# A transformer block on one core: the first queries from scaled weights, late rows and early modulates retimed, and attention's k, v and wq loads two steps later

## The chip, the cores and the metric

One NeuronCore of one Trainium2 chip. The metric is device time in microseconds (us). Engines: TensorE (PE; PEld is its weight load), VectorE (DVE), ScalarE (ACT), GpSimd (POOL), and SyncE (SP), whose instruction queue issues nearly all DMAs here.

## The reference, cut to what matters

```python
def reference(A_x, A_k_cache, A_v_cache, A_wq, A_wo, B_x, B_w_in, B_w_sp, B_b_sp, B_w_out, c, w_mod):
    mod = (_silu(c) @ w_mod).reshape(c.shape[0], 6, 1, -1)      # w_mod is (1024, 6144)
    sa, ca, ga, sb, cb, gb = ...                                 # six rows of 1024
    h = _layernorm(x) * (1 + ca) + sa                            # x is (1, 2048, 1024)
    x = x + ga * attention(h)       # q = h @ wq; 32 heads of 128; k and v cached, 2048 keys; @ wo
    h = _layernorm(x) * (1 + cb) + sb
    x = x + gb * gated_mlp(h)       # GELU, layernorm, token mixing by w_sp, w_out
    return x
```

All tensors are bf16. Before the first query exists the kernel needs x normalised, the columns sa and 1 + ca (a 4 MB part of w_mod times one vector), and wq.

## The kernel before

Attention runs as 64 "halves" of 16 steps: a half is one head and 1024 of the 2048 queries, a step is 128 keys. Halves 0 to 15 take heads 0 to 7 (first 1024 queries of each, then the rest); later, two halves per head. Each step is two score matmuls, one exponential on ScalarE, two matmuls with v, and a running sum `pacc` on VectorE, with one matmul of the next queries as filling. The first 1024 rows of x are normalised, transposed and modulated before attention; the other eight rows of tiles ("late rows") are done on VectorE during halves 0 to 6.

```python
    load_wm(nc.scalar, 0, 1)                       # w_mod in 512 KB blocks of 256 columns
    load_wm(nc.scalar, 1, 1)
    for ti in range(8):
        nc.sync.dma_start(xg[ti // 2][:, ti % 2], x_dram[:, ti, :])
    load_wm(nc.sync, 0, 0)
    ...                                            # k0, more w_mod, wq and v, mixed
    def q_work(h, qh, new_ps=side_ps):             # queries of one half, in 16 matmuls
        ...
                nc.tensor.matmul(box["ps"][:], wq_t[:, dc, hc:hc + DH],
                                 h1T[:, dc, q0:q0 + 512],
                                 start=(dc == 0), stop=(dc == KD - 1))
    ...
    def late_rows(g):                              # g counts steps from 0 to 1023
        ti, r = 8 + (g - 4) // 12, (g - 4) % 12
        if g == 0:
            load_row(8)
        if 4 <= g < 100:
            if r == 0:   ...                       # statistics of one row of tiles, next load
            elif r == 2: ...                       # normalise, store
            elif r == 6: ...                       # load back transposed, into h1T
        elif 100 <= g < 108:
            modulate(g - 100, 1024, 1024)
    ...
    for g, (i, kb) in enumerate(steps):            # i is the half, kb the step in it
        ...
        if kb == 2 and i < 16:
            load_kv(halves[i + 1][0])              # kT (a DMA transpose) and v
            if i == 12:
                load_wq(2)                         # 1 MB
        elif kb == 2 and qh == 0 and h + 1 < H:
            load_kv(h + 1)
            if h % 4 == 2 and h + 2 < H:
                load_wq((h + 2) // 4)
        ...                                        # the matmuls, the exponential, the sum
        if i > 0:
            work = ({13: finish_here, 15: load_rec} if i <= 8 else
                    {0: store_sums, 3: turn_sums, 10: finish_den, 13: load_rec}).get(kb)
            if work:
                work(i - 1)                        # the softmax denominators of the half before
```

From half 9 on, the denominators take a way through DRAM: the sums are stored (step 0), loaded back by a DMA transpose as `pT` (`turn_sums`, step 3), reduced on VectorE as `den` (`finish_den`, step 10), and their reciprocals go out and come back broadcast as `rbc`.

The softmax here doesn't subtract the row's maximum and nothing guards it: scores larger than these inputs give would overflow.

Of the kernel before, what the change touches and what calls it, by code (L numbers as in the profile page):

```python
# [16 lines left out]
def kernel(  # L17
# [42 lines left out]
    def wide_ps(name, shape=(P, 1024), dtype=FP32):  # L60
        return psum.tile(list(shape), dtype, name=name, tag="wide", bufs=2)

    def bank_ps(name, shape, dtype=FP32):
        return psum.tile(shape, dtype, name=name, tag="bank", bufs=3)
# [35 lines left out]

    c_sb = early.tile([KD, P], BF16, name="c_sb")
    nc.sync.dma_start(c_sb[:], c.rearrange("o (kc p) -> (o kc) p", p=P))
    xg, wms = [], []
    for j in range(4):
        xg.append(early.tile([P, 2, D], BF16, name=f"xg{j}"))
        wms.append(early.tile([P, 2, KD, 256], BF16, name="wm", tag="wm", bufs=4))

    def load_wm(eng, j, k):
        eng.dma_start(wms[j][:, k], wmod_v[:, :, k * D + j * 256:k * D + (j + 1) * 256])


    k0 = early.tile([P, NKB, DH], BF16, name="k0")
# [4 lines left out]
    kts[0] = att.tile([P, S], BF16, name="kT", tag="kT", bufs=2)  # L117
    vs[0] = att.tile([P, NKB, DH], BF16, name="v_sb", tag="v_sb", bufs=2)
    nc.scalar.activation(small.tile([P, 1], FP32, name="warm_e")[:], eps_tile[:], ACT.Exp)
    load_wm(nc.scalar, 0, 1)  # L120
    load_wm(nc.scalar, 1, 1)
    for ti in range(8):
        nc.sync.dma_start(xg[ti // 2][:, ti % 2], x_dram[:, ti, :])
    load_wm(nc.sync, 0, 0)
    load_wm(nc.sync, 1, 0)
    nc.sync.dma_start(k0[:], A_k_cache[0, 0].rearrange("(p j) d -> p j d", p=P))
    load_wm(nc.sync, 2, 0)
    nc.sync.dma_start(wq_g[0][:, :, 0:256], wq_v[:, :, 0:256])
    load_wm(nc.sync, 3, 0)
    nc.sync.dma_start(vs[0][:], A_v_cache[0, 0].rearrange("(p j) d -> p j d", p=P))  # L130
    nc.sync.dma_start(wq_g[0][:, :, 256:512], wq_v[:, :, 256:512])

    def ln_stats(chunks):

# [34 lines left out]
    def silu():  # L169

        nc.tensor.transpose(cT_ps[:], c_sb[:, :], identity[:KD, :KD])
        nc.scalar.activation(e_sb[:], cT_ps[:], ACT.Exp, scale=-1.0)
        load_wm(nc.scalar, 2, 1)
        load_wm(nc.scalar, 3, 1)

    def silu_end():
        nc.vector.tensor_scalar_add(out=e_sb[:], in0=e_sb[:], scalar1=1.0)
# [11 lines left out]

    mpss = {}  # L190

    def mod_products(j):
        mps = mpss[j] = bank_ps("mps", [P, 2, 2])
        for k in range(2):
            for f in range(2):
                for kc in range(KD):
                    nc.tensor.matmul(mps[:, k, f:f + 1], wms[j][:, k, kc, f * P:(f + 1) * P],
                                     scT[:, kc:kc + 1], start=(kc == 0), stop=(kc == KD - 1))

    def mod_columns(j):  # L200
        mps = mpss.pop(j)
        nc.vector.tensor_copy(out=cols[:, 0, 2 * j:2 * j + 2], in_=mps[:, 0, :])
        nc.vector.tensor_scalar_add(out=cols[:, 1, 2 * j:2 * j + 2], in0=mps[:, 1, :],
                                    scalar1=1.0)

    def modulate(dc, t0, n, eng=nc.vector, src=None):

        dst = h1T[:, dc, t0:t0 + n]
        if src is None:
            src = dst  # L210
        else:
            dst = dst.rearrange("p (t k) -> p t k", k=P)
        if eng is nc.scalar:
            nc.scalar.activation(dst, src, ACT.Identity, bias=cols[:, 0, dc:dc + 1],
                                 scale=cols[:, 1, dc:dc + 1])
            return
        nc.vector.tensor_scalar(out=dst, in0=src, scalar1=cols[:, 1, dc:dc + 1],
                                scalar2=cols[:, 0, dc:dc + 1], op0=ALU.mult, op1=ALU.add)

    row, junk = {}, early.tile([P, D], BF16, name="junk")  # L220

    def stats_act(ti):

# [19 lines left out]
        nc.gpsimd.tensor_tensor(out=rstd[:], in0=var[:], in1=neg_half[:], op=ALU.pow)  # L243
        row[ti] = (mv, rstd)

    turned_x = {}

    def turn(j, evacuate=True):
        hps = turned_x[j] = wide_ps("hps", [P, KD, 2, P], BF16)
        for t in range(2):  # L250
            for dc in range(KD):
                nc.tensor.transpose(hps[:, dc, t, :],
                                    xg[j][:, t, dc * P:(dc + 1) * P], identity[:])
        if evacuate:
            nc.scalar.activation(
                h1T[:, :, j * 256:(j + 1) * 256],
                hps[:].rearrange("p d t k -> p d (t k)"), ACT.Copy)

    def dve(ti):
        row[ti] = row_stats(xg[ti // 2][:, ti % 2, :])  # L260
# [20 lines left out]
    norm(1)  # L281
    turn(0)
    keep_busy(4)
    mod_products(0)
    finish_act(2)
    stats_act(5)
    dve(4)
    norm(2)
    norm(3)
    turn(1)  # L290
    mod_columns(0)
    mod_products(1)
    keep_busy(4)
    dve(6)
    norm(4)
    finish_act(5)
    dve(7)
    norm(5)
    turn_k(0)
    turn(2)  # L300
    mod_columns(1)
    mod_products(2)
    norm(6)
    norm(7)
    turn(3, False)
    k_late = turn_k(1, False)
    keep_busy(2)
    mod_products(3)
    mod_columns(2)
    for dc in range(4):  # L310
        modulate(dc, 0, 768)
    for dc in (4, 5):
        modulate(dc, 0, 768)
        modulate(dc, 768, 256, nc.scalar, turned_x[3][:, dc, :, :])
    mod_columns(3)
    modulate(6, 0, 768)
    modulate(7, 0, 768, nc.scalar)
    for dc in range(4):
        modulate(dc, 768, 256, nc.vector, turned_x[3][:, dc, :, :])
    for dc in (6, 7):  # L320
        modulate(dc, 768, 256, nc.scalar, turned_x[3][:, dc, :, :])
    k_late()


    wo_v = A_wo.rearrange("(h p) n -> p h n", p=P)
# [13 lines left out]
    def q_work(h, qh, new_ps=side_ps):  # L339

        out_t = att.tile([P, 1024], BF16, name="qT", tag="qT", bufs=3)
        qts[(h, qh)] = out_t
        wq_t = wq_g[h // 4]
        hc = (h % 4) * DH
        work = []
        for j in range(2):
            box = {}

            def one(dc, j=j, box=box):
                if dc == 0:  # L350
                    box["ps"] = new_ps("qps", [P, 512])
                q0 = qh * 1024 + j * 512
                nc.tensor.matmul(box["ps"][:], wq_t[:, dc, hc:hc + DH],  # L353
                                 h1T[:, dc, q0:q0 + 512],
                                 start=(dc == 0), stop=(dc == KD - 1))
                if dc == KD - 1:
                    nc.vector.tensor_copy(out=out_t[:, j * 512:(j + 1) * 512],  # L357
                                          in_=box["ps"][:])
            for dc in range(KD):
                work.append(lambda dc=dc, one=one: one(dc))  # L360
        return work


# [14 lines left out]
        s_tiles[g] = sps  # L378

    nc.sync.dma_start(wq_g[1][:], wq_v[:, :, 512:1024])  # L380
    for fn in q_work(0, 0, bank_ps):
        fn()
    emit_s(0)
    emit_s(1)
# [86 lines left out]

    def late_rows(g):

        ti, r = 8 + (g - 4) // 12, (g - 4) % 12
        if g == 0:
            load_row(8)
        if 4 <= g < 100:
            if r == 0:
                rows[ti] += row_stats(rows[ti][0][:, :]),
                if ti + 1 < NT:  # L480
                    load_row(ti + 1)
            elif r == 2:
                xt, st = rows.pop(ti)
                hb = early.tile([P, D], BF16, name="hb1", tag="hb1", bufs=2)
                centre(xt[:, :], st, hb[:])
                nc.sync.dma_start(h1_dram[ti % 2], hb[:])
            elif r == 6:
                nc.sync.dma_start(out=h1T[:, :, ti * P:(ti + 1) * P], in_=h1_dram[ti % 2],
                                  transpose=True)
        elif 100 <= g < 108:  # L490
            modulate(g - 100, 1024, 1024)

    def load_row(ti):
        rows[ti] = (early.tile([P, D], BF16, name="xt", tag="xt", bufs=2),)
        nc.sync.dma_start(rows[ti][0][:], x_dram[:, ti, :])

    wm_l = {}
    cols_l = early.tile([P, 32], FP32, name="cols_l")

    def late_mods(i, kb):  # L500
# [1 line left out]

        n0, odd = divmod(i - 17, 2)
        if n0 < 8 and not odd and kb == 2:
            wm_l[n0] = early.tile([P, KD, 512], BF16, name="wm_l", tag="wm", bufs=4)
            nc.sync.dma_start(wm_l[n0][:], wmod_v[:, :, (n0 + 4) * 512:(n0 + 5) * 512])
        elif n0 < 8 and not odd and kb == 14:
            wm = wm_l.pop(n0)
            mod_ps = side_ps("mod_ps", [P, 4])
            for f in range(4):  # L510
                for kc in range(KD):
                    nc.tensor.matmul(mod_ps[:, f:f + 1], wm[:, kc, f * P:(f + 1) * P],
                                     scT[:, kc:kc + 1], start=(kc == 0), stop=(kc == KD - 1))
            nc.vector.tensor_scalar_add(out=cols_l[:, 4 * n0:4 * n0 + 4], in0=mod_ps[:],
                                        scalar1=1.0 if n0 // 2 == 2 else 0.0)
        elif i == 33 and kb == 2:
            turned = early.tile([P, 32], FP32, name="turned_l")
# [12 lines left out]
    for g, (i, kb) in enumerate(steps):  # L530
# [10 lines left out]
        if kb == 2 and qh == 1 and 20 <= h < 28:  # L541
            k = 4 * (h - 20)
            nc.sync.dma_start(wo_t[:, k:k + 4, :], wo_v[:, k:k + 4, :])
        if kb == 2 and i < 16:
            load_kv(halves[i + 1][0])
            if i == 12:
                load_wq(2)
        elif kb == 2 and qh == 0 and h + 1 < H:
            load_kv(h + 1)
            if h % 4 == 2 and h + 2 < H:  # L550
                load_wq((h + 2) // 4)
# [233 lines left out]
```

## Time and profile before

| | |
|---|---|
| time, median of 12 runs | 1871.03 us (1867.56 to 1873.41) |
| span of the profiled run | 1869.1 us |
| TensorE busy | 1831.2 us (98%) |
| first exponential of attention | 32.97 us |
| a half without stalls | 17.29 us (80 matmuls, 216 ns apart) |

I cut attention into halves by the start of each half's first exponential, read from the timeline. Most halves take 17.29 us; eight of the halves 17 to 32 take 18.07 because they also hold 32 small matmuls for later modulation columns. The following stood out:

```
half          2      5      6      12     20     21     28     36     52
us            19.02  19.22  18.19  17.88  21.14  19.05  19.14  18.35  18.17
without stall 17.29  17.29  17.29  17.29  18.07  17.29  18.07  17.29  17.29
```

Four views of the kernel before follow. First, the page: busy us of each engine with its share of the span and instruction count.

```profile
PE 1831.2 (98%) x8830; PEld 845.9 (45%) x8995; DVE 1261.6 (68%) x2110; ACT 1105.0 (59%) x1167; POOL 32.8 (2%) x55
```

Second, the chain of waits around the worst stall (start us, us, what).

```profile
392.24 1.36 SPq L329
393.60 0.05 issue
393.65 10.14 DMA pT<-sums_dram
403.79 0.02 issue
403.81 1.23 DVE den L418
...
406.74 0.38 PE sps L374
```

TensorE's score matmul at 406.74 can be followed back to a DMA of 10.14 us. The issues on the sync queue in that stretch (timeline: start, us, engine, line, operation) say why:

```profile
389.12 0.36 SPq L406 DMA_DIRECT2D sums_dram<-pacc  x1
389.58 1.98 SPq L334 DMA_TRANSPOSE kT<-in_A_k_cache_dram  x1
391.65 0.53 SPq L336 DMA_DIRECT2D v_sb<-in_A_v_cache_dram  x1
392.24 1.36 SPq L329 DMA_DIRECT2D wq_t<-in_A_wq_dram  x1
393.65 4.60 SPq L411 DMA_TRANSPOSE pT<-sums_dram  x1
```

The pT transpose goes out behind kT, v and wq, 2 MB in all. By the completion semaphores in the trace they landed in the order of issue: kT at 393.72, v at 396.04, wq at 401.20 and pT at 403.79. The waits from 190 to 1150 us (total us, times, longest us) say how often this holds VectorE:

```profile
DVE den L418 <- DMA pT<-sums_dram: 15.4, 7, 4.4
```

Seven times, 4.4 us at worst. Third, the start, from the timeline: the last normalise, the last block of w_mod, the column products that wait for it, the first exponential.

```profile
15.51 4.54 SPq L109 DMA_DIRECT2D wm<-in_w_mod_dram  x1
...
21.48 1.16 DVE L151 TENSOR_SCALAR xg<-xg,mv,rstd 128x1024 bf16<-128x1024 bf16 x2
...
27.29 0.95 PE L197 MATMUL mps<-scT,wm 128*128 128x1 bf16 x32 [0.77 <-DMA wm<-in_w_mod_dram]
...
32.97 2.85 ACT L555 ACTIVATE pt<-sps 128x1024 bf16<-128x1024 f32 x3 [0.71 <-PE sps L374]
```

Fourth, windows of halves 0, 1, 20 and 21: length, then busy us (and instructions) of PE, PEld, DVE, ACT and POOL, the granted clock of TensorE, the DMA share and GB/s.

```profile
32.97:50.40 17.43, 16.68 (x76) 7.50 (x77) 12.10 (x21) 15.84 (x17) 0.86 (x1) 1.00 0.44 113
50.40:67.89 17.49, 17.38 (x87) 7.92 (x88) 14.85 (x27) 15.97 (x18) 0.93 (x1) 1.00 0.45 106
386.02:407.16 21.14, 18.03 (x111) 8.55 (x112) 14.47 (x24) 16.17 (x18) 0.00 (x0) 1.00 0.73 162
407.16:426.21 19.05, 19.00 (x81) 8.30 (x81) 16.01 (x27) 16.05 (x17) 0.00 (x0) 0.91 0.41 125
```

In half 21 the granted clock is 0.91: the trace's clock records show half speed from 407.4 to 410.9 us, just after the stall (128x512 matmuls start 427 ns apart there).

### The profile page before, as it was taken

How to read it: one execution, taken by the hardware profiler on the slowest of the kernel's cores; microseconds unless marked ns; L12 is line 12 of the kernel's file. 1: busy time of each engine (PE TensorE's matmuls, PEld its weight loads, DVE VectorE, ACT ScalarE, POOL GpSimd, SP SyncE). 2: the span in 40 equal slices, each digit the busy share in tenths (PEclk: the TensorE clock that was granted, in tenths of full speed). 3: DMA queues.
4: the chain of work that ended last, by engine and by line, in shares of the span. 5: the costliest groups of instructions: out<-in, count | busy, mean ns of one | idle time of the engine just before them, and what ended most of it. 6: DMA issues, size and time to landing. Idle time of an engine off the chain costs nothing.

```text
span 1869.1 us, 24473 instructions
## 1 busy us (share of the span) xinstructions
PE 1831.2 (98%) x8830; PEld 845.9 (45%) x8995; DVE 1261.6 (68%) x2110; ACT 1105.0 (59%) x1167; POOL 32.8 (2%) x55
## 2 busy tenths in 40 slices
PE   6999999999999999999999999999999999999999
PEld 4444444444444444444444444444445444444444
DVE  6898888878888988888888888444455400333334
ACT  6889999988988989999999997000013332000000
POOL 1000000000000000000000000000000000000000
PEclk9999999999999999999999999999999999999999
DMA  8465465464564643564564433766433012221102
GB/s 248 120 169 118 128 156 153 124 153 123 132 172 116 164 122 99 142 167 127 136 167 131 109 108 112 226 206 157 116 88 87 12 46 79 51 56 40 46 1 79
DMA packets 404346, 223.68 MB, mean 120 GB/s; under 512 B 302592, under 2 KB 359936, under 8 KB 404224
## 3 DMA queue, kind: packets, MB, share of 16 engines
q1 hardware_dynamic: 400064, 220.01, 44.3%
q10 hardware_dynamic: 4160, 2.10, 0.4%
q8 instruction: 70, 1.15, 0.3%
q14 instruction: 52, 0.43, 0.1%
HBM read 126.88 MB, written 45.63 MB: 92 GB/s over the span
## 4 chain that ended last, share of the span: by engine, by line
PE 89%; DVE 4%; DMA 4%; issue 1%; SPq 1%; ACT 0%; POOL 0%; DVEq 0%; ACTq 0%; POOLq 0%
PE ops L567 20%; PE sps L374 20%; PE acc L466 12%; PE qps L353 10%; PE gps L714 10%; PE zps L664 5%; PE bo L735 5%; PE zps L697 5%; DMA pT<-sums_dram 3%; DVE pacc L577 2%; DMA wm<-in_w_mod_dram 1%; SPq L329 0%; DVE den L418 0%; DVE qT L357 0%; ACT pt L555 0%
## 5 line engine op out<-in xcount | busy, mean ns | idle before, releaser
L555 ACT ACTIVATE pt<-sps 128x1024 bf16<-128x1024 f32 x1024 | 1018.7, 1025 | 107.8 <-PE sps L374 78.5
L577 DVE TENSOR_TENSOR pacc<-pacc,pt 128x1024 bf16<-128x1024 bf16 x896 | 616.8, 688 | 63.2 <-ACT pt L555 4.0
L374 PE MATMUL sps<-qT,kT 128*128 128x512 bf16 x1999 | 600.3, 379 | 7.9 <-DVE qT L357 6.9
L567 PE MATMUL ops<-pt,v_sb 128*128 128x512 bf16 x1993 | 598.1, 379 | 6.2 <-DVE ou L573 1.3
L353 PE MATMUL qps<-h1T,wq_t 128*128 128x512 bf16 x1022 | 344.2, 380 | 2.1 <-DVE rec L431 1.2
L567 PEld LDWEIGHTS <-v_sb 128*128 128x128 bf16 x2048 | 200.2, 98 | 250.3 <-issue 9.7
L374 PEld LDWEIGHTS <-kT 128*128 128x128 bf16 x2048 | 199.1, 98 | 245.8 <-issue 9.7
L466 PE MATMUL acc<-wo_t,ot 128*128 128x512 bf16 x972 | 215.7, 379 | 1.1
L666 ACT ACTIVATE z<-zps 128x448 bf16<-128x448 f32 x64 | 34.8, 544 | 283.3 <-PE zps L664 280.4
L714 PE MATMUL gps<-wsp,z 128*128 128x512 bf16 x878 | 192.9, 379 | 0.9
L717 DVE TENSOR_TENSOR g<-gps,b_bc 128x512 bf16<-128x512 f32 x56 | 38.7, 692 | 222.1 <-PE gps L714 215.2
L353 PEld LDWEIGHTS <-wq_t 128*128 128x128 bf16 x1024 | 100.2, 98 | 121.2 <-issue 0.8
L466 PEld LDWEIGHTS <-ot 128*128 128x128 bf16 x992 | 97.0, 98 | 116.8
L714 PEld LDWEIGHTS <-z 128*128 128x128 bf16 x896 | 87.7, 98 | 105.7
L357 DVE CAST qT<-qps 128x512 bf16<-128x512 f32 x128 | 88.4, 691 | 42.3 <-PE qps L353 41.2
L735 PE MATMUL bo<-w_out_t,z1T 128*128 128x512 bf16 x439 | 96.7, 379 | 0.5
L664 PE MATMUL zps<-z2w,h2T 128*128 128x448 bf16 x512 | 97.0, 352 | 0.0
L697 PE MATMUL zps<-h2T,z1w 128*128 128x512 bf16 x439 | 96.4, 379 | 0.5
L643 DVE TENSOR_TENSOR tmp<-acc,ga 128x512 f32<-128x512 f32 x32 | 22.0, 688 | 100.2 <-PE acc L466 100.2
L418 DVE TENSOR_REDUCE den<-pT 128x8 f32<-128x1024 bf16 x55 | 65.3, 1187 | 15.4 <-DMA pT<-sums_dram 15.4
L440 DVE TENSOR_TENSOR oT<-ou,rbc 128x1024 bf16<-128x1024 f32 x62 | 75.6, 1219 | 0.2 <-DMA rbc<-rec_dram 0.2
L664 PEld LDWEIGHTS <-h2T 128*128 128x128 bf16 x512 | 50.1, 98 | 46.8
(82 smaller groups left out, 649.3 us busy)
## 6 DMA issues: line engine op xcount, KB each, us to landing
rbc<-rec_dram SPq DMA_DIRECT2D x64, 512.0 KB
v_sb<-in_A_v_cache_dram SPq DMA_DIRECT2D x40, 512.0 KB
oT_dram<-oT SPq DMA_DIRECT2D x62, 256.0 KB
sums_dram<-pacc SPq DMA_DIRECT2D x55, 256.0 KB
ot<-oT_dram SPq DMA_DIRECT2D x24, 512.0 KB
wm_l<-in_w_mod_dram SPq DMA_DIRECT2D x8, 1024.0 KB
wo_t<-in_A_wo_dram SPq DMA_DIRECT2D x8, 1024.0 KB
wq_t<-in_A_wq_dram SPq DMA_DIRECT2D x7, 1024.0 KB
```

Source lines behind the costliest of these rows:

```text
L353: nc.tensor.matmul(box["ps"][:], wq_t[:, dc, hc:hc + DH], h1T[:, dc, q0:q0 + 512], start=(dc == 0), stop=(dc == KD - 1))
L357: nc.vector.tensor_copy(out=out_t[:, j * 512:(j + 1) * 512], in_=box["ps"][:])
L374: nc.tensor.matmul(sps[:, j * 512:(j + 1) * 512], kts[h][:, kb * P:(kb + 1) * P], qts[(h, qh)][:, j * 512:(j + 1) * 512], start=True, stop ...
L440: nc.vector.tensor_mul(out=oT[:], in0=state[i]["ou"][:], in1=state[i]["rbc"][:])
L466: nc.tensor.matmul(accs[ti][:, sl], lhs, wo_t[:, hh, sl], start=(hh == 0), stop=(hh == H - 1))
L555: nc.scalar.activation(pt[:], s_tiles.pop(g)[:], ACT.Exp, scale=SCALE)
L567: nc.tensor.matmul(o_ps[j][:], vs[h][:, kb, :], pt[:, j * 512:(j + 1) * 512], start=(kb == 0), stop=(kb == NKB - 1))
L577: nc.vector.tensor_add(out=pacc[:], in0=pacc[:], in1=pt[:])
L664: nc.tensor.matmul(zps[:], h2T[:, dc, ti * P:(ti + 1) * P], z2w[:, dc, sl], start=(dc == 0), stop=(dc == KD - 1))
L697: nc.tensor.matmul(zps[:], w[:, dc, :], h2T[:, dc, q * 512:(q + 1) * 512], start=(dc == 0), stop=(dc == KD - 1))
L714: nc.tensor.matmul(gps[:], z2[s][:, f * P:(f + 1) * P], wsps[q][:, s, :], start=(s == 0), stop=(s == NT - 1))
L735: nc.tensor.matmul(bo[:], z1T[:, f, ti * P:(ti + 1) * P], w_out_t[:, f, sl], start=(f == 0), stop=(f == NF - 1))
```

## The change

Its intent is to begin attention before the modulation is done. Since (n * (1 + ca) + sa) @ wq = n @ ((1 + ca) * wq) + sa @ wq, the first two heads' queries of the first 1024 rows are made from unmodulated rows `xnT` with scaled weights `wqs`, and the shift `q_add` is added when the result is copied out of PSUM, the buffer that the matmuls write. The rows that later heads need are modulated in steps 2 to 9 of half 0. w_mod comes in 1 MB blocks of 512 columns behind x; `keep_busy(n)` issues n dummy matmuls on zeros, whose result nobody uses, to keep TensorE busy; the late rows start at step 14 and follow every 11 steps; and the k, v and wq loads of attention move from step 2 to step 4 of a half.

```diff
-    load_wm(nc.scalar, 0, 1)
-    load_wm(nc.scalar, 1, 1)
     for ti in range(8):
         nc.sync.dma_start(xg[ti // 2][:, ti % 2], x_dram[:, ti, :])
-    load_wm(nc.sync, 0, 0)
-    load_wm(nc.sync, 1, 0)
+    nc.sync.dma_start(wq_g[0][:, :, 0:256], wq_v[:, :, 0:256])
     nc.sync.dma_start(k0[:], A_k_cache[0, 0].rearrange("(p j) d -> p j d", p=P))
     ... (the rest of w_mod, v and wq are issued after the small exponential of silu)
+    def scale_wq(j):
+        for dc in range(4 * j, 4 * j + 4):
+            ... (wqs = wq * (1 + ca): four on ScalarE, four on VectorE)
+    def query_shift():
+        ... (16 matmuls of one column: qs = wq^T sa; q_add = qs)
     ... (start of attention)
-    turn(3, False)
-    k_late = turn_k(1, False)
-    keep_busy(2)
+    turn(3, (0, 1))
+    scale_wq(0)
+    turn_k(1)
+    keep_busy(4)
     mod_products(3)
-    ... (16 modulates on VectorE and ScalarE)
+    mod_columns(3)
+    scale_wq(1)
+    keep_busy(8)
+    mod_products(0)
+    mod_columns(0)
     ...
-    for fn in q_work(0, 0, bank_ps):
+    first = q_work(0, 0, bank_ps)
+    for fn in first[:7]:
+        fn()
+    mod_products(1)
+    mod_columns(1)
+    query_shift()
+    for fn in first[7:]:
         fn()
     ...
-        ti, r = 8 + (g - 4) // 12, (g - 4) % 12
+        ti, r = 8 + (g - 14) // 11, (g - 14) % 11
         if g == 0:
             load_row(8)
-        if 4 <= g < 100:
+        if 2 <= g < 10:
+            modulate(h1T, xnT, g - 2)
+        elif 14 <= g < 102:
     ...
-        elif 100 <= g < 108:
-            modulate(g - 100, 1024, 1024)
+        elif 102 <= g < 110:
+            late = h1T[:, :, 1024:]
+            modulate(late, late, g - 102)
     ...
-        if kb == 2 and i < 16:
+        if kb == 4 and i < 16:
             load_kv(halves[i + 1][0])
             if i == 12:
                 load_wq(2)
-        elif kb == 2 and qh == 0 and h + 1 < H:
+        elif kb == 4 and qh == 0 and h + 1 < H:
             load_kv(h + 1)
```

More of the change, by code (lines that the diff above doesn't have):

```diff
@@ L102, with load_wm @@
     nc.sync.dma_start(c_sb[:], c.rearrange("o (kc p) -> (o kc) p", p=P))
-    xg, wms = [], []
+    xg, wms = [], {}
     for j in range(4):
         xg.append(early.tile([P, 2, D], BF16, name=f"xg{j}"))
-        wms.append(early.tile([P, 2, KD, 256], BF16, name="wm", tag="wm", bufs=4))
-    def load_wm(eng, j, k):
-        eng.dma_start(wms[j][:, k], wmod_v[:, :, k * D + j * 256:k * D + (j + 1) * 256])
+    def load_wm(eng, n0):
+        wms[n0] = early.tile([P, KD, 512], BF16, name="wm", tag="wm", bufs=4)
+        eng.dma_start(wms[n0][:], wmod_v[:, :, n0 * 512:(n0 + 1) * 512])
     k0 = early.tile([P, NKB, DH], BF16, name="k0")
@@ L119 @@
     nc.scalar.activation(small.tile([P, 1], FP32, name="warm_e")[:], eps_tile[:], ACT.Exp)
-    load_wm(nc.scalar, 0, 1)
-    load_wm(nc.scalar, 1, 1)
     for ti in range(8):
         nc.sync.dma_start(xg[ti // 2][:, ti % 2], x_dram[:, ti, :])
-    load_wm(nc.sync, 0, 0)
-    load_wm(nc.sync, 1, 0)
+    nc.sync.dma_start(wq_g[0][:, :, 0:256], wq_v[:, :, 0:256])
     nc.sync.dma_start(k0[:], A_k_cache[0, 0].rearrange("(p j) d -> p j d", p=P))
-    load_wm(nc.sync, 2, 0)
-    nc.sync.dma_start(wq_g[0][:, :, 0:256], wq_v[:, :, 0:256])
-    load_wm(nc.sync, 3, 0)
-    nc.sync.dma_start(vs[0][:], A_v_cache[0, 0].rearrange("(p j) d -> p j d", p=P))
-    nc.sync.dma_start(wq_g[0][:, :, 256:512], wq_v[:, :, 256:512])
     def ln_stats(chunks):
@@ L172, in silu @@
         nc.scalar.activation(e_sb[:], cT_ps[:], ACT.Exp, scale=-1.0)
-        load_wm(nc.scalar, 2, 1)
-        load_wm(nc.scalar, 3, 1)
+        load_wm(nc.scalar, 2)
+        load_wm(nc.scalar, 3)
+        load_wm(nc.sync, 0)
+        load_wm(nc.sync, 1)
+        nc.sync.dma_start(vs[0][:], A_v_cache[0, 0].rearrange("(p j) d -> p j d", p=P))
+        nc.sync.dma_start(wq_g[0][:, :, 256:512], wq_v[:, :, 256:512])
     def silu_end():
@@ L190 @@
     mpss = {}
-    def mod_products(j):
-        mps = mpss[j] = bank_ps("mps", [P, 2, 2])
-        for k in range(2):
-            for f in range(2):
-                for kc in range(KD):
-                    nc.tensor.matmul(mps[:, k, f:f + 1], wms[j][:, k, kc, f * P:(f + 1) * P],
-                                     scT[:, kc:kc + 1], start=(kc == 0), stop=(kc == KD - 1))
-    def mod_columns(j):
-        mps = mpss.pop(j)
-        nc.vector.tensor_copy(out=cols[:, 0, 2 * j:2 * j + 2], in_=mps[:, 0, :])
-        nc.vector.tensor_scalar_add(out=cols[:, 1, 2 * j:2 * j + 2], in0=mps[:, 1, :],
-                                    scalar1=1.0)
@@ L206, in modulate @@
-    def modulate(dc, t0, n, eng=nc.vector, src=None):
-        dst = h1T[:, dc, t0:t0 + n]
-        if src is None:
-            src = dst
-        else:
-            dst = dst.rearrange("p (t k) -> p t k", k=P)
-        if eng is nc.scalar:
-            nc.scalar.activation(dst, src, ACT.Identity, bias=cols[:, 0, dc:dc + 1],
-                                 scale=cols[:, 1, dc:dc + 1])
-            return
-        nc.vector.tensor_scalar(out=dst, in0=src, scalar1=cols[:, 1, dc:dc + 1],
-                                scalar2=cols[:, 0, dc:dc + 1], op0=ALU.mult, op1=ALU.add)
@@ L220, with mod_products, mod_columns @@
-    row, junk = {}, early.tile([P, D], BF16, name="junk")
+    def mod_products(n0, new_ps=bank_ps):
+        mps = mpss[n0] = new_ps("mps", [P, 4])
+        for f in range(4):
+            for kc in range(KD):
+                nc.tensor.matmul(mps[:, f:f + 1], wms[n0][:, kc, f * P:(f + 1) * P],
+                                 scT[:, kc:kc + 1], start=(kc == 0), stop=(kc == KD - 1))
+    def mod_columns(n0):
+        k, j = divmod(n0, 2)
+        nc.vector.tensor_scalar_add(out=cols[:, k, 4 * j:4 * j + 4], in0=mpss.pop(n0)[:],
+                                    scalar1=float(k))
@@ new lines, in modulate @@
+    def modulate(dst, src, dc):
+        nc.vector.tensor_scalar(out=dst[:, dc, 0:1024], in0=src[:, dc, 0:1024],
+                                scalar1=cols[:, 1, dc:dc + 1], scalar2=cols[:, 0, dc:dc + 1],
+                                op0=ALU.mult, op1=ALU.add)
+    xnT = early.tile([P, KD, 1024], BF16, name="xnT")
+    wqs = early.tile([P, KD, 2 * DH], BF16, name="wqs")
+    shift = early.tile([P, KD], BF16, name="shift")
+    q_add = early.tile([P, 2], FP32, name="q_add")
+    def scale_wq(j):
+        for dc in range(4 * j, 4 * j + 4):
+            if j == 0:
+                nc.scalar.activation(wqs[:, dc, :], wq_g[0][:, dc, 0:256], ACT.Identity,
+                                     scale=cols[:, 1, dc:dc + 1])
+            else:
+                nc.vector.tensor_scalar(out=wqs[:, dc, :], in0=wq_g[0][:, dc, 0:256],
+                                        scalar1=cols[:, 1, dc:dc + 1], scalar2=None,
+                                        op0=ALU.mult)
@@ new lines, in query_shift @@
+    def query_shift():
+        qs = side_ps("qs", [P, 2])
+        nc.vector.tensor_copy(out=shift[:], in_=cols[:, 0, :])
+        for h in range(2):
+            for dc in range(KD):
+                nc.tensor.matmul(qs[:, h:h + 1], wq_g[0][:, dc, h * DH:(h + 1) * DH],
+                                 shift[:, dc:dc + 1], start=(dc == 0), stop=(dc == KD - 1))
+        nc.vector.tensor_copy(out=q_add[:], in_=qs[:])
+    row = {}
+    junk = early.tile([P, D], BF16, name="junk", tag="hb1", bufs=2)
@@ L244, in finish_act, with turn @@
         row[ti] = (mv, rstd)
-    turned_x = {}
-    def turn(j, evacuate=True):
-        hps = turned_x[j] = wide_ps("hps", [P, KD, 2, P], BF16)
+    def turn(j, evacuate=(2,)):
+        hps = wide_ps("hps", [P, KD, 2, P], BF16)
         for t in range(2):
@@ L253, in turn @@
                                     xg[j][:, t, dc * P:(dc + 1) * P], identity[:])
-        if evacuate:
-            nc.scalar.activation(
-                h1T[:, :, j * 256:(j + 1) * 256],
-                hps[:].rearrange("p d t k -> p d (t k)"), ACT.Copy)
+        for eng in evacuate:
+            dcs = {2: slice(0, KD), 0: slice(0, 4), 1: slice(4, KD)}[eng]
+            dst = xnT[:, dcs, j * 256:(j + 1) * 256]
+            src = hps[:, dcs].rearrange("p d t k -> p d (t k)")
+            if eng:
+                nc.scalar.activation(dst, src, ACT.Copy)
+            else:
+                nc.vector.tensor_copy(out=dst, in_=src)
     def dve(ti):
@@ L283 @@
     keep_busy(4)
-    mod_products(0)
     finish_act(2)
@@ L290 @@
     turn(1)
-    mod_columns(0)
-    mod_products(1)
+    mod_products(2)
     keep_busy(4)
@@ L295 @@
     norm(4)
+    mod_columns(2)
     finish_act(5)
@@ L300 @@
     turn(2)
-    mod_columns(1)
-    mod_products(2)
     norm(6)
     norm(7)
-    turn(3, False)
-    k_late = turn_k(1, False)
-    keep_busy(2)
+    turn(3, (0, 1))
+    scale_wq(0)
+    turn_k(1)
+    keep_busy(4)
     mod_products(3)
-    mod_columns(2)
-    for dc in range(4):
-        modulate(dc, 0, 768)
-    for dc in (4, 5):
-        modulate(dc, 0, 768)
-        modulate(dc, 768, 256, nc.scalar, turned_x[3][:, dc, :, :])
-    mod_columns(3)
-    modulate(6, 0, 768)
-    modulate(7, 0, 768, nc.scalar)
-    for dc in range(4):
-        modulate(dc, 768, 256, nc.vector, turned_x[3][:, dc, :, :])
-    for dc in (6, 7):
-        modulate(dc, 768, 256, nc.scalar, turned_x[3][:, dc, :, :])
-    k_late()
+    mod_columns(3)
+    scale_wq(1)
+    keep_busy(8)
+    mod_products(0)
+    mod_columns(0)
     wo_v = A_wo.rearrange("(h p) n -> p h n", p=P)
@@ L342, in q_work @@
         qts[(h, qh)] = out_t
-        wq_t = wq_g[h // 4]
+        plain = h < 2 and qh == 0
+        wq_t, src = (wqs, xnT) if plain else (wq_g[h // 4], h1T)
         hc = (h % 4) * DH
@@ L347, in q_work, with one @@
             box = {}
-            def one(dc, j=j, box=box):
-                if dc == 0:
+            def one(n, j=j, box=box):
+                dc = (n + 4) % KD if plain else n
+                if n == 0:
                     box["ps"] = new_ps("qps", [P, 512])
@@ L353, in one @@
                 nc.tensor.matmul(box["ps"][:], wq_t[:, dc, hc:hc + DH],
-                                 h1T[:, dc, q0:q0 + 512],
-                                 start=(dc == 0), stop=(dc == KD - 1))
-                if dc == KD - 1:
+                                 src[:, dc, q0:q0 + 512],
+                                 start=(n == 0), stop=(n == KD - 1))
+                if n == KD - 1 and plain:
+                    nc.vector.tensor_scalar_add(out=out_t[:, j * 512:(j + 1) * 512],
+                                                in0=box["ps"][:], scalar1=q_add[:, h:h + 1])
+                elif n == KD - 1:
                     nc.vector.tensor_copy(out=out_t[:, j * 512:(j + 1) * 512],
                                           in_=box["ps"][:])
-            for dc in range(KD):
-                work.append(lambda dc=dc, one=one: one(dc))
+            for n in range(KD):
+                work.append(lambda n=n, one=one: one(n))
         return work
@@ L495, in load_row @@
         nc.sync.dma_start(rows[ti][0][:], x_dram[:, ti, :])
-    wm_l = {}
     cols_l = early.tile([P, 32], FP32, name="cols_l")
@@ L504, in late_mods @@
         if n0 < 8 and not odd and kb == 2:
-            wm_l[n0] = early.tile([P, KD, 512], BF16, name="wm_l", tag="wm", bufs=4)
-            nc.sync.dma_start(wm_l[n0][:], wmod_v[:, :, (n0 + 4) * 512:(n0 + 5) * 512])
+            load_wm(nc.sync, n0 + 4)
         elif n0 < 8 and not odd and kb == 14:
-            wm = wm_l.pop(n0)
-            mod_ps = side_ps("mod_ps", [P, 4])
-            for f in range(4):
-                for kc in range(KD):
-                    nc.tensor.matmul(mod_ps[:, f:f + 1], wm[:, kc, f * P:(f + 1) * P],
-                                     scT[:, kc:kc + 1], start=(kc == 0), stop=(kc == KD - 1))
-            nc.vector.tensor_scalar_add(out=cols_l[:, 4 * n0:4 * n0 + 4], in0=mod_ps[:],
+            mod_products(n0 + 4, side_ps)
+            nc.vector.tensor_scalar_add(out=cols_l[:, 4 * n0:4 * n0 + 4],
+                                        in0=mpss.pop(n0 + 4)[:],
                                         scalar1=1.0 if n0 // 2 == 2 else 0.0)
```

## The prediction

> **What bounds the kernel now.** TensorE: 1831 of 1869 us busy (page, part 1). Two parts of the 38 us of idle matter. (a) The start: the first softmax exponential of attention begins at 32.97 us (timeline); the chain of waits reaches it through the last 512 KB column block of w_mod, issued at 15.51, landed at 27.24. (b) Stalls in attention. Cutting the timeline at the first exponential of each head-half gives 17.29 us for most halves (80 matmuls, 216 ns apart), but 21.14 and 19.05 for halves 20 and 21. There the chain of waits shows a 10.14 us DMA transpose of the row sums (pT), issued at 393.65 behind kT, v and a 1 MB wq load; VectorE waits 4.4 us for it before "den", and the clock halves for 3.4 us afterwards. Halves 28, 36, 52 and 12 also load wq and are 0.6 to 1.1 us over.
>
> **What the change does.**
> 1. Start: the first two heads' queries for the first 1024 tokens use scaled weights on unmodulated rows; the shift is added at the evacuation. w_mod comes in 1 KB runs. Packet records: 512 B packets take 27 to 32 ns, 1 KB packets 45 ns, about a quarter more per engine. [...] x goes out ahead of w_mod and lands 1.5 to 4 us earlier; before, ScalarE was held issuing w_mod until 11.4 us, and VectorE waited 1.9 us for its statistics. Normalising should end near 18.5 us, not 22.6, and the last w_mod block land near 23.5, not 27.2. But TensorE's queue behind the last transposes grows: 12 dummy matmuls (was 2), two groups of column products (0.95 us each), a 1 us chain for the query shift, then nine query matmuls and an evacuation. These sum to about 13.5 us after the last normalise: first exponential near 32.4 us. Gain 0.6 us (-2 to +1.5).
> 2. Eight 128x1024 modulates (541 ns each, 4.3 us) move to half 0. VectorE limits halves 2 to 6: busy 46.3 of 50 us at 80 to 130 (windows), the chain there mostly its sums. Halves 0 and 1 have slack for about half. Cost 2.5 us (0.5 to 4.5).
> 3. kT/v/wq loads move from step 2 to step 4 of a half, behind the pT transpose (step 3) on the sync queue. The stalls of halves 20/21, 28, 36, 52 and 12 sum to 9.3 us above the floor. Most should go; the reciprocal's round trip (rec, rbc) now queues behind wq and may give some back. Gain 7.5 us (4 to 9.5).
>
> **Predicted:** 1872.5 - 0.6 + 2.5 - 7.5, about 1867 us, range 1861 to 1873. Chances: faster by over 2% 0.01, within 2% 0.985, slower 0.005.
>
> **What would show it.** Step 1: first exponential at 31 to 33 us, TensorE no longer waiting for w_mod last. Step 2: halves 0 to 6 together 127 to 131 us, not 126.4. Step 3: no wait of den for pT; halves 20 and 21 near 17.3 (plus 0.8 where column products fall).
>
> **What would make it wrong.** TensorE still cold at 20 us; kT, two steps later, arriving after step 14 in the first 16 halves, which would stall every one of them; VectorE having more room early than I count; or rbc arriving late enough that the pT stalls only change their name.

The packet times of step 1 in the packet records of the first 33 us: 512 B mostly 27 to 36 ns (mean 30.2, kernel before), 1 KB 46 to 55 ns (mean 48.5, kernel after), 17.0 and 21.1 B per ns, so a quarter more; in the kernel after alone, where the 512 B packets took 27.0 ns, it is a ninth more.

## The result, and the profile after

The kernel after takes 1859.65 us (median of 10 runs, 1859.19 to 1862.74), against 1871.03 us before. The ratio is 0.9942, with a 95% interval of 0.9933 to 0.9952: 0.6% faster, clear of noise and within the 2% that the classes use. Ratios here are the mean time of one kernel's runs over that of the other's of the same rounds, so not quite the ratio of the medians. The prediction, 1867 us with a range of 1861 to 1873, was too slow: the median lies 1.35 us under the range. The prediction started from 1872.46 us, the median of the first three runs of the kernel before; over all twelve the median is 1.4 us lower. About 5.5 us of gain were forecast and 11.4 us measured.

The two profiled spans, cut at the same places (the last half is cut at the start of its last exponential, here and below):

| part | before | after | change | predicted |
|---|---|---|---|---|
| start, to the first exponential | 32.97 | 31.21 | -1.76 | -0.6 |
| halves 0 to 8 | 161.30 | 161.05 | -0.25 | +2.5 |
| halves 9 to 63 | 963.35 | 954.25 | -9.10 | -7.5 |
| rest | 711.45 | 711.20 | -0.25 | 0 |
| span | 1869.1 | 1857.7 | -11.4 | -5.6 |

Now the lines that answer to those above. The page:

```profile
PE 1829.5 (98%) x8855; PEld 845.5 (46%) x9021; DVE 1263.0 (68%) x2110; ACT 1103.1 (59%) x1167; POOL 32.4 (2%) x55
```

The chain of waits around the same place in half 20, and the sync queue there:

```profile
388.97 0.43 PE sps L383 x2
389.40 0.43 PE ops L579 x2
390.05 0.43 PE sps L383 x2
```

The chain is TensorE alone now.

```profile
386.44 0.36 SPq L421 DMA_DIRECT2D sums_dram<-pacc  x1
388.50 1.25 SPq L426 DMA_TRANSPOSE pT<-sums_dram  x1
390.37 0.33 SPq L457 DMA_DIRECT2D oT_dram<-oT  x1
390.75 2.00 SPq L338 DMA_TRANSPOSE kT<-in_A_k_cache_dram  x1
392.80 0.57 SPq L340 DMA_DIRECT2D v_sb<-in_A_v_cache_dram  x1
393.41 1.30 SPq L333 DMA_DIRECT2D wq_t<-in_A_wq_dram  x1
```

The waits from 190 to 1150 us hold no wait of den for pT any more. VectorE's only wait for a DMA there is a new one, for the broadcast reciprocals:

```profile
DVE oT L455 <- DMA rbc<-rec_dram: 1.0, 1, 1.0
```

The pT transpose now goes out ahead of the 2 MB. By its completion semaphore in the trace it landed at 391.50, 3.0 us after its issue, against 10.1 us before. The start, from the timeline:

```profile
17.41 1.62 DVE L143 TENSOR_SCALAR xg<-xg,mv,rstd 128x1024 bf16<-128x1024 bf16 x3
...
22.02 1.89 PE L184 MATMUL zps<-zeros 128*128 128x512 bf16 x8
...
26.05 0.94 PE L193 MATMUL mps<-scT,wm 128*128 128x1 bf16 x32
...
31.21 2.85 ACT L567 ACTIVATE pt<-sps 128x1024 bf16<-128x1024 f32 x3 [7.23 <-PE sps L383]
```

The last normalise ends at 19.03 us, not 22.64. The column products at 26.05 no longer wait for w_mod (its last block landed at 25.46). In the chain of waits TensorE works through its own queue from 21.21 us on, the eight dummies at 22 us (1.75 us of the chain) included. The column products at 21.21 did wait 0.2 us for an earlier w_mod block, which landed at 21.16. In two more profiles with this start the chain goes back to that block as well, in three to the normalising, so the two are nearly tied. The gain of 1.76 us is from one pair of profiles: the first exponential came at 31.02 to 31.63 us in five more profiles with the same start, and at 32.80 to 33.14 in three more with the old one. Halves 0, 1, 20 and 21 in windows:

```profile
31.21:48.69 17.48, 16.75 (x77) 7.49 (x77) 13.63 (x24) 15.82 (x16) 0.00 (x0) 1.00 0.28 68
48.69:66.54 17.85, 17.46 (x87) 7.94 (x88) 16.35 (x31) 15.98 (x18) 1.78 (x2) 1.00 0.45 119
383.34:401.41 18.07, 17.96 (x112) 8.64 (x113) 15.33 (x26) 16.05 (x18) 0.00 (x0) 1.00 0.69 190
401.41:418.70 17.29, 17.18 (x80) 7.79 (x81) 15.16 (x25) 15.87 (x17) 0.00 (x0) 1.00 0.52 139
```

VectorE does 1.5 us more in half 0 and as much more in half 1, and the two halves together take 0.4 us longer. Halves 20 and 21 fell by 4.8 us.

### The profile page after: what moved, and what is told of

Same layout as the page of the kernel before. It is cut to its first block, busy times and chain, and to the rows that moved or that the text cites. A ratio compares the mean times of both kernels' runs of the same rounds, so it can differ in the third digit from the quotient of the medians. Undisturbed runs are those within 1.5% of the kernel's fastest.

```text
span 1857.7 us, 24527 instructions
## 1 busy us (share of the span) xinstructions
PE 1829.5 (98%) x8855; PEld 845.5 (46%) x9021; DVE 1263.0 (68%) x2110; ACT 1103.1 (59%) x1167; POOL 32.4 (2%) x55
## 3 DMA queue, kind: packets, MB, share of 16 engines
q8 instruction: 70, 1.15, 0.3%
## 4 chain that ended last, share of the span: by engine, by line
PE 94%; DVE 3%; issue 1%; DMA 1%; ACT 1%; SPq 0%; POOL 0%; DVEq 0%; POOLq 0%
PE ops L579 23%; PE sps L383 22%; PE acc L481 12%; PE qps L359 12%; PE gps L726 10%; PE zps L676 5%; PE bo L747 5%; PE zps L709 5%; DVE pacc L589 1%; DMA wm<-in_w_mod_dram 1%; ACT pt L567 1%; PE mps L193 0%; DVE stats L138 0%; DMA xg<-in_A_x_dram 0%; DVE oT L455 0%
## 5 line engine op out<-in xcount | busy, mean ns | idle before, releaser
L359 PE MATMUL qps<-h1T,wq_t 128*128 128x512 bf16 x988 | 334.3, 379 | 1.4 <-DVE rec L446 0.4
L711 ACT ACTIVATE z1T<-zps 128x512 bf16<-128x512 f32 x56 | 33.4, 597 | 63.3 <-PE zps L709 61.1
```

The costliest lines, as they stand in the source:

```text
L359: nc.tensor.matmul(box["ps"][:], wq_t[:, dc, hc:hc + DH], src[:, dc, q0:q0 + 512], start=(n == 0), stop=(n == KD - 1))
```

## The experiments

The theories were these. **Order:** the 9 us of halves 9 to 63 come from putting the loads behind the pT transpose on the sync queue. **Rivals:** they come with the new start or the retimed rows; or from the loads simply starting later. For halves 0 to 8: **limit** (my prediction's reading: VectorE is full, so added work is added time) against **slack** (VectorE's idle time in halves 0 and 1 takes it up).

### Only the loads moved

```diff
 (the kernel before)
-        if kb == 2 and i < 16:
+        if kb == 4 and i < 16:
-        elif kb == 2 and qh == 0 and h + 1 < H:
+        elif kb == 4 and qh == 0 and h + 1 < H:
```

> The kernel before, with nothing changed but the k/v/wq loads moved from step 2 to step 4 of a half. Theory A (order on the sync queue: the pT transpose of step 3 now goes out ahead of these loads): halves 9 to 63 lose their 9 us of stalls, halves 12, 20, 21, 28, 36, 52 fall to 17.3 (18.1 where column products fall), the start stays at 32.97 us, total about 1862 us, 9 us under the kernel before. Rival B (the 9 us came with the new start or with the retimed rows): under 3 us. Halves 0 to 8 tell whether this move alone changes them: no change expected, 161.3 us.

Measured: 1861.53 us against 1870.27 of the kernel before in the same rounds, ratio 0.995 (0.9937 to 0.9962). Halves 9 to 63 take 953.86 us; halves 12, 20, 21, 28, 36 and 52 are at 17.3 or 18.07. First exponential 33.14, halves 0 to 8 161.63. Order holds: this two-character edit brings 8.7 us.

### Everything but the move of the loads

```diff
 (the kernel after)
-        if kb == 4 and i < 16:
+        if kb == 2 and i < 16:
-        elif kb == 4 and qh == 0 and h + 1 < H:
+        elif kb == 2 and qh == 0 and h + 1 < H:
```

> The kernel after, with these loads put back to step 2. Theory A: the stalls of halves 12, 20, 21, 28, 36, 52 come back, total about 1869 us, 9 us over the kernel after, 2 us under the kernel before. Rival B: within 3 us of the kernel after. Halves 0 to 8: if the move of the loads had hidden a cost of the eight modulates, they grow from 161.05 by up to 2.5 us; if the modulates cost nothing by themselves, they stay within 1 us.

Measured: 1865.30 us, ratio to before 0.9969 (0.9957 to 0.9982). The stalls come back (half 20 at 20.47, half 36 at 18.45), but halves 9 to 63 take 960.25 us: 6.0 us above the kernel after, not 9. Part of the difference is half 21, 17.36 here and 19.05 before: here the clock did not fall after the stall (mean granted clock of the run 1.0, against 0.997). Halves 0 to 8 take 161.04 us, so the move of the loads hid nothing there.

### The loads at step 3

```diff
 (the kernel after)
-        if kb == 4 and i < 16:
+        if kb == 3 and i < 16:
-        elif kb == 4 and qh == 0 and h + 1 < H:
+        elif kb == 3 and qh == 0 and h + 1 < H:
```

> The kernel after, with these loads at step 3 instead of 4: in the program they then stand in the same step as the pT transpose, but ahead of it. Theory A (order): all the stalls come back as in the run with step 2, total about 1869 us. Rival C (what counts is how many steps later the loads start): about half the 9 us come back, total about 1864 us.

Measured: 1865.21 us, the same as with step 2; halves 9 to 63 take 959.57 us. In the program the loads of a step stand ahead of its `turn_sums`. So one step of delay brings nothing and the next brings it all: what counts is being behind pT. VectorE's waits of this run from 190 to 1150 us:

```profile
DVE den L433 <- DMA pT<-sums_dram: 13.2, 6, 3.3
```

### Only wq moved

```diff
 (the kernel before)
         if kb == 2 and i < 16:
             load_kv(halves[i + 1][0])
-            if i == 12:
-                load_wq(2)
         elif kb == 2 and qh == 0 and h + 1 < H:
             load_kv(h + 1)
-            if h % 4 == 2 and h + 2 < H:
-                load_wq((h + 2) // 4)
+        if kb == 4 and i == 12:
+            load_wq(2)
+        elif kb == 4 and i >= 16 and qh == 0 and h % 4 == 2 and h + 2 < H:
+            load_wq((h + 2) // 4)
```

> The kernel before, with only the wq loads moved behind the pT transpose (step 4), k and v left ahead of it at step 2. If the 1 MB of wq is what makes pT late: halves 12, 20, 21, 28, 36, 52 are back at 17.3 or 18.1, halves 9 to 63 take 954 to 955 us, total about 1862 us, as with the move of all three. If k and v alone delay it too: 1 to 5 us of the 9 remain.

Measured: 1862.00 us, ratio 0.9949 (0.9936 to 0.9963); halves 9 to 63 take 954.27 us, no wait of den for pT is left. The 1 MB of wq is the culprit. In half 20 of this run pT, issued behind kT and v at 392.13, landed after 4.8 us; den comes seven steps (about 7.6 us, at 17.29 us for 16 steps) later in the program, so 4.8 us cost nothing and 10.1 us did.

### The modulates of half 0 twice

```diff
 (the kernel after)
         if 2 <= g < 10:
             modulate(h1T, xnT, g - 2)
+            modulate(h1T, xnT, g - 2)
```

> The kernel after, with each of the eight modulates of half 0 done twice (same result): another 4.3 us on VectorE in steps 2 to 9. My prediction's reading (VectorE is the limit of halves 0 to 6, so work added there is time added): halves 0 to 8 grow by 3 to 4.3 us, to about 165. Rival (VectorE has room in half 0, and what is over is caught up later): they grow by 0 to 1 us.

Measured: halves 0 to 8 take 163.76 us, 2.7 us more; total 1862.17 us. Half 0 grows to 19.16 and half 1 to 18.88, the others do not change. Between the two expectations: a second 4.3 us no longer fits.

### No modulates in half 0

```diff
 (the kernel after; wrong on purpose)
-        if 2 <= g < 10:
-            modulate(h1T, xnT, g - 2)
+        if g == 2:
+            nc.gpsimd.memset(h1T[:, :, 0:1024], 0.0)
```

> Wrong result on purpose: the kernel after without the eight modulates of half 0 (GpSimd writes zeros into those columns instead, off VectorE). It measures what these 4.3 us cost in place. My prediction's step 2: halves 0 to 8 shrink by about 2.5 us from 161.05. Slack theory (half 0 holds 4.3 us of idle VectorE time that is used up first; the second 4.3 us of the doubled run cost 2.7): they shrink by 0.5 us or less, half 0 stays at 17.4 to 17.5.

Measured: halves 0 to 8 take 161.03 us, with the modulates 161.05. In place they cost nothing. (The result check reported this run as correct, so it is not sharp enough to notice these columns.) The total, 1867.72 us, is of no use, because my edit spoiled the start: nothing made the zeros wait for step 2, so GpSimd wrote them at 18.48 us, right after its last row statistics. The timeline of this run:

```profile
17.58 8.15 DVE L143 TENSOR_SCALAR xg<-xg,mv,rstd 128x1024 bf16<-128x1024 bf16 x3
...
18.48 6.97 POOL L493 MEMSET h1T<- 128x8192 bf16 x1
```

Three normalises that take 1.62 us in the kernel after took 8.15 us beside it, and the first exponential came at 40.11. Whether the memset held them, and how, no run shows.

### The kernel after with the late rows at their old steps

```diff
 (the kernel after)
-        ti, r = 8 + (g - 14) // 11, (g - 14) % 11
+        ti, r = 8 + (g - 4) // 12, (g - 4) % 12
         if 2 <= g < 10:
             modulate(h1T, xnT, g - 2)
-        elif 14 <= g < 102:
+        if 4 <= g < 100:
 ...
-        elif 102 <= g < 110:
+        elif 100 <= g < 108:
-            modulate(late, late, g - 102)
+            modulate(late, late, g - 100)
```

> The kernel after, with the eight late rows at their old steps (first at step 4, every 12 steps, their modulates at 100 to 107) and the early modulates kept at 2 to 9. If the retimed rows made the room for the modulates: half 0 has both and grows by 1 to 2 us, halves 2, 5 and 6 look like the kernel before (19.0, 19.2, 18.2), halves 0 to 8 are 162.5 to 163.5 us. If the row times do not matter: 161 us.

Measured: halves 0 to 8 take 162.95 us, half 0 17.72. Total 1860.02 us, against 1859.65 of the kernel after, which is within the spread of these runs.

### The kernel before with the late rows retimed

```diff
 (the kernel before)
-        ti, r = 8 + (g - 4) // 12, (g - 4) % 12
+        ti, r = 8 + (g - 14) // 11, (g - 14) % 11
-        if 4 <= g < 100:
+        if 14 <= g < 102:
-        elif 100 <= g < 108:
-            modulate(g - 100, 1024, 1024)
+        elif 102 <= g < 110:
+            modulate(g - 102, 1024, 1024)
```

> The kernel before, with only the late rows retimed as in the kernel after (first at step 14, every 11 steps, modulates at 102 to 109). If retiming pays by itself: halves 0 to 8 fall from 161.3 to about 160 us. If it only pushes the same work later (my prediction: rows crowd halves 1 to 6): they grow to 161.5 to 163. Nothing else changes, total 1869 to 1872 us.

Measured: halves 0 to 8 take 161.25 us, total 1869.93 us, ratio 0.9996. So retiming alone brings nothing. It moves stalls (half 2 from 19.02 to 17.47, half 3 from 17.47 to 18.30) and leaves their sum. Half 0 of this run in a window:

```profile
32.80:50.22 17.42, 16.74 (x78) 7.51 (x77) 10.36 (x16) 15.82 (x17) 0.00 (x0) 1.00 0.28 68
```

VectorE is busy for 10.36 us there, 7.1 us idle; the kernel after puts its eight modulates there (541 ns each, 4.3 us; the busy time grows by 3.3 us only, to 13.63, because records of neighbouring instructions overlap, by 0.08 to 0.09 us around the modulates of the kernel after) and half 0 takes 17.48 us. Together, for halves 0 to 8:

```
modulates in half 0   late rows at old steps        late rows at new steps
none                  161.30 (before)               161.25, 161.03
eight                 162.95                        161.05 (after)
sixteen               not run                       163.76
```

The left column is less sharp than it looks: three more runs with old row times and no modulates gave 161.63, 161.91 and 162.30 us. With new row times and eight modulates, four more runs gave 161.02 to 161.04. So at the old row times the modulates cost 0.7 to 1.7 us, on one run, and at the new ones none.

### Without the eight dummy matmuls

```diff
 (the kernel after)
     scale_wq(1)
-    keep_busy(8)
     mod_products(0)
```

> The kernel after without the eight dummy matmuls before the shift's first column products. If TensorE's own queue sets the first exponential (after: 31.21 us): it comes 0.5 to 0.6 us earlier, then held by the last w_mod block landing near 25.5 us. If the dummies keep the clock up (full from 13.9 us in the kernel after): the clock falls to half in the start and the exponential comes later than 31.2 us.

Measured: 1859.25 us (1858.66 to 1862.22), no different from the kernel after. The profiled run was the longest of the four (1862.22), with the exponential at 33.93. w_mod came late in it (TensorE waited 1.6 us for it at 23.12), and the clock records show half speed from 25.2 to 32.0. Windows of 25 to 32 us, of this run:

```profile
25.00:32.00 7.00, 6.54 (x62) 3.22 (x61) 1.49 (x6) 0.00 (x0) 0.00 (x0) 0.51 1.23 269
```

and of the kernel after:

```profile
25.00:32.00 7.00, 5.45 (x65) 2.99 (x66) 2.00 (x5) 0.79 (x1) 0.00 (x0) 1.00 1.15 303
```

Inconclusive as to the mean. The half speed of the profiled run lasts 6.8 us, twice the 3.4 us after the stall of half 20 in the kernel before. In the 3.4 us before the fall TensorE was busy for 2.0 us (1.75 of it one-column products), and its one long idle stretch was 1.6 us. That the dummies guard against the fall is not shown: w_mod landed later in this run as well (its last block at 26.42 us, against 25.46), and one of the ten runs of the kernel after, with its dummies, took 1862.74 us.

### The kernel before with x ahead of w_mod

```diff
 (the kernel before)
-    load_wm(nc.scalar, 0, 1)
-    load_wm(nc.scalar, 1, 1)
     for ti in range(8):
 ...
         nc.scalar.activation(e_sb[:], cT_ps[:], ACT.Exp, scale=-1.0)
+        load_wm(nc.scalar, 0, 1)
+        load_wm(nc.scalar, 1, 1)
         load_wm(nc.scalar, 2, 1)
         load_wm(nc.scalar, 3, 1)
```

> The kernel before, with the two first w_mod loads of the scalar queue issued after the small exponential instead of ahead of x, nothing else changed. x should land 1 to 4 us earlier and the last normalise end near 19 to 20 us instead of 22.64. If the start of the kernel before is set by the w_mod bytes (last block landed at 27.24): the first exponential stays at 32.5 to 33.5 us. If it is set by the normalising: it comes 2 to 3 us earlier. Total 1868 to 1873 us in the first case.

Measured: 1871.92 us, ratio 1.0004. x landed 1.2 to 3.2 us earlier, but the normalising ended at 24.59, later than before, which I had not expected: ScalarE was now held issuing four blocks until 13.4 us, and its share of the row statistics came late. From the waits of 0 to 34 us:

```profile
ACT junk L226 <- DMA wm<-in_w_mod_dram: 10.9, 1, 10.9
```

The last w_mod block landed at 27.82 and the first exponential came at 33.88. So x ahead of w_mod does not help by itself; the run cannot say which of the two late ends, normalising or w_mod, held it.

### Six buffers for the exponentials

```diff
 (the kernel after)
-        pt = att.tile([P, 1024], BF16, name="pt", tag="pt", bufs=5)
+        pt = att.tile([P, 1024], BF16, name="pt", tag="pt", bufs=6)
```

> The kernel after with six instead of five buffers for the exponentials' output, which lets VectorE's sums fall one step further behind before ScalarE stops. If the 5.4 us that halves 0 to 8 take over 17.29 each come from short backlogs of VectorE: they shrink by 1 to 2 us, total 1858 to 1859 us. If they come from evacuations that TensorE itself waits for (the ou copies at a half's end, the query evacuation): no change, 161 us.

Measured: 1859.38 us, halves 0 to 8 161.04 us, half by half the same. The 5.4 us above 17.29 per half are not the exponential's buffers running out. No version that I ran beats the kernel after by more than its noise.

## Why the prediction was right or wrong

**Direction and mechanism of the main gain: right.** The loads' move was forecast to remove the waits of den for pT and did; running it alone gave 8.7 us, and running everything else left the stalls. I credited it with 7.5 us of the 9.3 I had counted, fearing that the reciprocals behind wq would give some back. (The count was itself too high: against the table above, the stalls of halves 12, 20, 21, 28, 36 and 52 sum to 8.4 us. The rest of the gain is in smaller excesses: 0.1 to 0.2 us each in halves 13, 29, 34, 37, 44, 45 and 53.) The measured 9.1 us and a single 1.0 us wait for rbc show that they gave back next to nothing.

**"Cost 2.5 us (0.5 to 4.5). Halves 0 and 1 have slack for about half": this step failed.** The cost measured was nothing: 161.05 us with the modulates, 161.03 without. "VectorE having more room early than I count", one of the prediction's own grounds for being wrong, is what happened. I read that VectorE was the limit in halves 2 to 6 and charged the work put into half 0 at that rate. But half 0 had 5.3 us of idle VectorE, and the change also takes the first late row out of it (7.1 us idle in the run with only the rows retimed). The 4.3 us fitted whole. A second 4.3 us did cost 2.7. The prediction does not mention the retimed rows at all; what I expected of them, as said before the run with them alone, was that the row pushed out of half 0 would crowd the later halves. It cost nothing: in that run halves 0 to 8 stayed at 161.25 us. My reading of halves 1 to 6 as simply full was wrong too. They fell from 108.95 to 107.97 us although VectorE does 1.2 us more in them. At the old row times a cost does show, 0.7 to 1.7 us, in one run; by that run, the change's retiming is what removes it.

**"First exponential near 32.4 us. Gain 0.6 us": mis-sized.** It came at 31.21, a gain of 1.76. Normalising ended at 19.03 (forecast 18.5) and the last w_mod landed at 25.46 (forecast 23.5), both later than I said. The error was in the sum behind the normalise, 13.5 us, which measured 12.2 (in this profile the chain of waits comes from a w_mod block landed at 21.16, not from the normalise). (18.5 and 13.5 give 32.0, not 32.4.) A likely reason is the clock, of which the prediction only says that TensorE might still be cold at 20 us (the kernel before had half speed there, from 18.3 to 25.2 us). At half speed the 128x512 dummies start 427 ns apart (before, at 20.6 us), at full speed 215 ns (after, at 22 us). In the clock records TensorE ran at full speed from 13.9 us on in the kernel after (its dummies at 11.1 us, ahead of the first record, start 427 ns apart), and from 13.2 to 15.9 in five more profiles with its start; with the old start (five profiles) full speed came for good only at 23.7 to 25.2 us. The start was not split further by a run, so how much the clock gave is not shown.

**Sum of the errors:** -1.2 (start), -2.8 (halves 0 to 8), -1.6 (halves 9 to 63) and -0.25 (rest). The modulates' cost is the largest.

**Left open.** How large the stalls are without the move varies from run to run: halves 9 to 63 took 959.6 to 963.4 us in five such profiles. In two of them (before, and before with rows retimed) the clock fell for 3.4 us behind the stall of half 20; in three it did not. In every profile the clock records show full or half speed only, and the changes lie whole multiples of 3.413 us apart, on a grid that begins elsewhere in each run (1.26 us after the start of the span in the kernel before, 0.21 in the kernel after). Laid over the stall of half 20, this grid gives a stretch in which TensorE was busy for 0.7 and 1.15 of the 3.41 us in the two profiles where the clock then fell; in the other three the least busy stretch had 1.47, 2.05 and 2.13 us. In the run without the dummies it fell after 2.0 us, so the busy time of such a stretch does not sort these cases by itself, and that the clock is judged by it is not shown. Nor does the length of the stall alone decide it: half 20 was 2.3 us over in one that fell and 2.4 in one that did not. No run set the position of the grid on purpose. The two parts run alone (8.7 and 5.0 us) sum to 2.3 us more than the whole; that halves 9 to 63 took 3.1 us less in the profile without the move (960.25) than in that of the kernel before (963.35) would account for it. What holds the 5.4 us left in halves 0 to 8 is open as well; six buffers did not touch it.

## What to carry to other kernels

On a queue whose transfers land in the order of issue, as those of the sync queue did in half 20 (kT at 393.72 us, pT last at 403.79, kernel before), put the small transfer that somebody waits for ahead of the bulk load that nobody needs for a long time: there a 256 KB transpose took 3.0 us from issue to landing with no bulk load before it in the half, 4.8 us behind 1 MB, and 10.1 us behind 2 MB (8.3 to 9.2 us in four more profiles with that order). Where the issues of one step stand in the program matters more than the step's number. Before charging moved work as added time, look up the idle time of that engine in the very stretch where the work lands, and in the stretch it leaves, rather than in the stretch where the engine is known to be full. The stall of half 20 was followed by 3.4 us at half speed in two of five profiles, and half 21 then took 19.05 us (kernel before) instead of 17.29, so a stall's true cost is read from the half after it too.
